# The experts' weight loads issued by ScalarE on a queue of its own, and the last token tile finished in two column halves

## The chip, the cores and the metric

The kernel runs on one core of one Trainium2 chip. The metric is the device time of one execution in microseconds. Before the change three runs took 833.31, 834.32 and 835.25 us, so the median is 834.32 us.

## What is computed

Three blocks follow one another, all in float32, for 2 batches of 576 tokens (1152 tokens) and a model width of 512.

```python
# attention: 8 heads of 64, with a bias that depends on positions
scores = q @ k.T / 8 + bias          # bias[i, j] = relu(log1p|i-j| / log1p(max(i,1)) * w1 + b1) @ w2
attn = softmax(scores); x = attn @ v
# experts: 4 of them, D = 512, F = 1024, every token goes through all, weighted by p
out = sum_e p[:, e] * (relu(x @ w1[e]) @ w2[e])
# gated block: d_ff = 1536
y = ((out @ w_a) * (out @ w_b)) @ w_out
```

## The kernel before, in words

**Numbers.** Matrix products run as three products of a high and a low part (hi*hi, hi*lo, lo*hi), so every operand is split: a cast gives the high part, a subtraction the low part.

**Order.** The order of instructions on each engine is not written down by hand. Every piece of work is an `op` with an estimated cost per engine, a priority (lower goes first) and the buffers it needs. `Plan.run` (line 137) plays the kernel through with these costs when the program is built. Whenever an engine is free in that play, it takes the ready op with the lowest priority whose buffers fit (at equal priority the one that has been ready longest), and the instruction is emitted there and then. On the chip each engine runs its own list in that order, and semaphores make it wait for data and for buffers. DMA transfers are modelled as one line of transfers one after another, at 250 bytes per ns and 1.9 us of latency (`DMA_RATE`, `DMA_LAT`, lines 92 and 93). In that play a DMA costs its issuing engine SyncE (SP) 440 ns. All DMAs of the kernel are issued by SP, so they stand in one hardware queue.

**Stages.** First the bias is made: 36 groups of 16 rows (`bias_group`), each with four hidden-layer tiles `hh` (VectorE L356 or ScalarE L358), eight matmuls `pb` (L370), a copy out of PSUM into `bst` (L388) and a store to a table `bias_d` in DRAM (L405). Attention runs in groups of one or more tiles of 128 query rows (`step`): a tile of bias rows `bt` is loaded from `bias_d` (L458), scores go to `ps` (TensorE L490), VectorE adds the bias and takes the maximum (L493), ScalarE takes the exponential (L503), TensorE transposes the result into `pt` (L516), and `pv` (L581) multiplies by the values. The first eight groups are the 128-row tiles 0 and 1 of the first batch. Tile 1 needs the bias rows up to 255, so it can load only after the sixteenth store.

The experts fill TensorE beside the rest of attention and go on alone after it. Each of 64 units of weights is brought by `unit` (line 615): a 512 KB load into a staging tile `wst` (L617), a cast `wh` (`whi`, on ScalarE or VectorE, L234), a subtraction `wl` (`wlo`, VectorE, L619). There are two staging tiles and, until the bias is finished, four pairs of `w` tiles. So two loads can be in flight, the third load waits until the first staging tile has been read by its `wl`, and no more than six loads can be issued before the first expert product has used its weights. The load has priority 2, the lowest, among SP's ops; the split has priority 1. `early` holds the eighth bias store: in the play no weight load starts before that store has landed. The up products are `up` (L708), the ReLU `hh` and `hl` (L735, L736), the down products `pz` (L719).

The 64-bit weights of the gated block are converted beside the experts and written to DRAM, then read again (`wz_d`). The gated block itself has seven products per pair of blocks (L834), sums on ScalarE and VectorE, and a down product. For the last pair (`out_item`, line 896) the down product of each token tile is emitted in two halves of the inner dimension (L911), then VectorE adds it to the accumulator (L916, 512 columns) and SP stores 256 KB (L920). The last tile, rows 1024 to 1151, is one contiguous run of output rows, so it is one store.

Of the kernel before, what the change touches and what calls it, by code (L numbers as in the profile page):

```python
# [13 lines left out]
ALU = mybir.AluOpType  # L14
# [5 lines left out]
P = 128  # L20
# [21 lines left out]
QUICK, BY_AGE, MARGIN, LATE = 0.9, True, 300, True  # L42
# [46 lines left out]
class Plan:  # L89
# [9 lines left out]
    def op(self, eng, fn, r=(), w=(), rw=(), hold=(), prio=0, lock=False, after=(), size=0):  # L99

        o = Op()
        o.eng, o.fn, o.prio, o.lock, o.size = eng, fn, prio, lock, size
        o.after, o.n, o.done = [], len(self.ops), False
        deps = set(after)
        for b in r:
            deps.update(b.writers)
        for b in rw:
            deps.update(b.writers)
            deps.update(b.readers)
        for b in rw:  # L110
            b.writers, b.readers = [o], []
        for b in w:
            b.writers.append(o)
        for b in r:
            b.readers.append(o)
        deps.discard(o)
        o.left = len(deps)
        for d in deps:
            d.after.append(o)
        o.bufs = list({id(b): b for b in (*r, *w, *rw, *hold)}.values())  # L120
        for b in o.bufs:
            b.left += 1
        self.ops.append(o)
        return o
# [12 lines left out]
    def run(self):  # L137
        ready = {e: [] for e in self.ENG}
        until = dict.fromkeys(self.ENG, 0.0)
        locked = {"DVE": 0.0, "POOL": 0.0}  # L140
        events, now, dma, left, count = [], 0.0, 0.0, len(self.ops), 0
        issued = set()

        def arrive(o, t):
            o.since = t
            for e in o.eng:
                ready[e].append(o)

        for o in self.ops:
            if not o.left:  # L150
                arrive(o, 0.0)
        while left:
            again = True
            while again:
                again = False
                for e in self.ENG:
                    if until[e] > now:
                        continue
                    ready[e] = [o for o in ready[e] if o.n not in issued]
                    best = None  # L160
                    fill = e == "PE" and MARGIN and any(o.prio >= 2 and self.fits(o) for o in ready[e])
                    for o in ready[e]:
                        if best is not None and (o.prio, o.since if BY_AGE else 0, o.n) >= (best.prio, best.since if BY_AGE else 0, best.n):
                            continue
                        if e == "PE" and o.prio < 2 and now < o.since + MARGIN and fill:
                            continue
                        other = {"DVE": "POOL", "POOL": "DVE"}.get(e)
                        if o.lock and other and locked[other] > now:
                            continue

                        if o.prio < QUICK and any(max(until[x], now) + o.eng[x] < now + o.eng[e] for x in o.eng if x != e):
                            continue
                        if self.fits(o):
                            best = o
                    if best is None:
                        continue
                    o = best
                    for b in sorted((b for b in o.bufs if b.t is None), key=lambda b: b.turn):
                        b.place = b.room.free.pop(0)
                        b.room.given += 1  # L180
                        b.t = b.place[0](b.name)
                    o.fn(e)
                    issued.add(o.n)
                    ns = o.eng[e]
                    until[e] = now + ns
                    if e == "SP":
                        dma = max(dma, now + ns + 400) + o.size / self.DMA_RATE
                        end = dma + self.DMA_LAT - 400
                    else:
                        end = now + ns + self.SETTLE[e]  # L190
                        if o.lock and e in locked:
                            locked[e] = now + ns + 50
                    heapq.heappush(events, (until[e], -1, None))
                    heapq.heappush(events, (end, count, o))
                    count += 1
                    again = True
            if not left:
                break
            assert events, ("stuck", [(o.n, list(o.eng), [(b.name, b.t is None) for b in o.bufs]) for e in self.ENG for o in ready[e]][:20])
            now = events[0][0]  # L200
            while events and events[0][0] <= now:
                _, _, o = heapq.heappop(events)
                if o is None:
                    continue
                left -= 1
                o.done = True
                for x in o.after:
                    x.left -= 1
                    if not x.left:
                        arrive(x, now)  # L210
                for b in o.bufs:
                    b.left -= 1
                    if not b.left and b.room is not None:
                        b.room.left -= 1
                        if b.place[1] in b.room.drop:
                            b.room.gone += 1
                        else:
                            b.room.free.append(b.place)
                for x in list(self.watch):
                    if x[0]():  # L220
                        self.watch.remove(x)
                        x[1]()
        return now
# [3 lines left out]
def tile_kernel(ctx, tc, qd, kd, vd, cst, probs, w1r, w2r, war, wbr, wor, out):  # L227
    nc = tc.nc
    plan = Plan()
    op = plan.op  # L230
# [114 lines left out]
    rows, early = [], []  # L345
# [268 lines left out]

    def unit(src):
        wst, w = new("wst"), new("w")
        op({"SP": 440}, lambda e: nc.sync.dma_start(out=wst.t, in_=src.rearrange("p a b -> p (a b)")), w=[wst], prio=2, size=524288, after=early if LATE else [])  # L617
        op(t_copy(1024, ENGINES["whi"]), lambda e: copy(e, w.t[0], wst.t), r=[wst], w=[w], prio=RANK["split"], lock=True)
        op(t_two(1024, ENGINES["wlo"]), lambda e: engine[e].tensor_tensor(out=w.t[1], in0=wst.t, in1=f(w.t[0]), op=ALU.subtract), r=[wst], rw=[w], prio=RANK["split"], lock=True)  # L619
        return w  # L620
# [67 lines left out]
    acc_t, ACC = {}, [Buf(t=x_hi) for _ in range(TOK)]  # L688
    late = {}

    def acc(t):
        if t not in acc_t:
            acc_t[t] = (mid if t < 2 else late["ap"]).tile([P, DM], F32, tag=f"acc{t}", name=f"acc{t}", bufs=1)
        return acc_t[t]
# [201 lines left out]
    def out_item(q, c, h):  # L896
        if (q, "d") not in WU:
            WU[q, "d"] = unit64(UI[q, "d"])
        for tt in range(4 + c):
            t = 4 * c + tt  # L900
            z = new("z", "pz")
            if (q, c) != AB[-1]:
                down(WU[q, "d"], z, h, tt, True, True, after=gap)
            else:

                halves = []
                for ft in (1, 0):
                    def mm(e, ft=ft, z=z, tt=tt):
                        wh, wl = (x.rearrange("p (a b) -> p a b", a=2) for x in WU[q, "d"].t)
                        for j, (a, bb) in enumerate(((h.t[0], wh), (h.t[1], wh), (h.t[0], wl))):  # L910
                            nc.tensor.matmul(z.t, a[:, ft, tt * P:(tt + 1) * P], bb[:, ft, :], start=(ft == 1 and j == 0), stop=(ft == 0 and j == 2))  # L911
                    halves.append(op({"PE": 3 * 226}, mm, r=[WU[q, "d"]], w=[z], hold=[h], prio=RANK["fill"], after=[*parts[q, c, ft], *halves]))
            if q == 0:
                op({"ACT": 600}, lambda e, z=z, t=t: nc.scalar.copy(acc(t), z.t), r=[z], rw=[ACC[t]], prio=RANK["evac2"])
            else:
                op({"DVE": 745}, lambda e, z=z, t=t: nc.vector.tensor_tensor(out=acc(t), in0=z.t, in1=acc(t), op=ALU.add), r=[z], rw=[ACC[t]], prio=RANK["evac2"])  # L916
            if q == NQ - 1:
                def put(e, t=t):
                    for r, o, n in rows_of(t):
                        nc.sync.dma_start(out=out[o:o + n, :], in_=acc(t)[r:r + n])  # L920
                op({"SP": 440 * len(rows_of(t))}, put, r=[ACC[t]], size=262144)
# [174 lines left out]
```

## Time and profile before

| | us |
|---|---|
| median of three runs | 834.32 |
| the profiled execution, its own time | 834.46 |
| its span, first to last instruction | 832.7 |
| TensorE busy (x4890) | 806.7 |
| VectorE busy (x1221) | 626.3 |
| ScalarE busy (x687) | 349.8 |
| GpSimd busy (x72) | 52.1 |
| weight loads `wst<-in_w1r`, `wst<-in_w2r` | 64, 512.0 KB each |

The profile is of one execution. PE is TensorE's matmuls, PEld its weight loads into the array, DVE is VectorE, ACT is ScalarE, SPq is SyncE's sequencer, which issues the DMAs. A row of a timeline gives the start, the length, the engine, the line, the operation and the names of what is written and read; in brackets stands how long the engine had been idle before it and what ended that. The issue of a DMA isn't counted as busy time of its engine. The chain of work that ended last is followed back from the last instruction. It stands for what set the time.

### The profile page before, as it was taken

To read this page: it belongs to the slowest core of one execution; us is meant where nothing else is said; L and a number is where in the kernel's file an instruction comes from. 1 tells how busy PE (TensorE), PEld (TensorE's weight loads), DVE (VectorE), ACT (ScalarE), POOL (GpSimd) and SP (SyncE) were. 2 spreads that over 40 slices of the span, in tenths; PEclk is the share of its full clock that TensorE was granted. 3 is DMA by queue.
4 is the path that set the end of the run, shared out by engine and by line. 5 is a ranking of instruction groups with operands and counts; after the bars stand their busy time and mean duration, and the time that the engine had idled before them with its cause. 6 is when DMAs were issued, how large, how long until landed. Compare 5 with 4: busy or idle time off the path is not lost.

```text
span 832.7 us, 12785 instructions
## 1 busy us (share of the span) xinstructions
PE 806.7 (97%) x4890; PEld 672.2 (81%) x4890; DVE 626.3 (75%) x1221; ACT 349.8 (42%) x687; POOL 52.1 (6%) x72
## 2 busy tenths in 40 slices
PE   7778999999999999999999999999999999999998
PEld 2346776898897788889888988888889999899996
DVE  7998999688888768787888787976266655747545
ACT  6677877477666621132122213113235432324211
POOL 1001100000110000000000000002003001100000
PEclk9999999999999999999999999999999999999999
DMA  6989877675756444556465545640202211211103
GB/s 220 313 285 340 279 256 240 202 235 184 226 176 209 135 159 126 182 174 206 115 202 190 165 140 177 215 127 23 79 1 71 83 58 45 76 27 50 52 1 113
DMA packets 48445, 128.13 MB, mean 154 GB/s; under 512 B 5120, under 2 KB 9216, under 8 KB 48384
## 3 DMA queue, kind: packets, MB, share of 16 engines
q1 hardware_dynamic: 48384, 127.32, 47.5%
q8 instruction: 38, 0.62, 0.3%
q14 instruction: 23, 0.19, 0.1%
HBM read 101.46 MB, written 25.84 MB: 153 GB/s over the span
## 4 chain that ended last, share of the span: by engine, by line
PE 90%; DVE 5%; DMA 3%; ACT 1%; issue 1%; DVEq 0%
PE pz L719 32%; PE up L708 24%; PE pw L834 9%; PE ps L490 5%; PE pv L581 4%; PE pr L834 4%; PE pt L516 4%; PE pq L834 2%; PE pb L370 2%; DMA k<-in_kd 1%; DVE hh L356 1%; DMA bt<-bias_d 1%; PE pz L911 1%; PE px L798 1%; DVE ptb L234 1%
## 5 line engine op out<-in xcount | busy, mean ns | idle before, releaser
L719 PE MATMUL pz<-wh,hh 128*128 128x512 f32 x386 | 153.9, 399 | 0.0
L719 PE MATMUL pz<-wl,hh 128*128 128x512 f32 x386 | 152.3, 395 | 0.0
L719 PE MATMUL pz<-wh,hl 128*128 128x512 f32 x386 | 151.6, 393 | 0.0
L708 PE MATMUL up<-x_hi,wh 128*128 128x256 f32 (+2 forms) x384 | 133.2, 347 | 0.4 <-DVE hl L736 0.4
L708 PE MATMUL up<-x_hi,wl 128*128 128x256 f32 (+2 forms) x384 | 129.8, 338 | 0.0
L708 PE MATMUL up<-x_lo,wh 128*128 128x256 f32 (+2 forms) x384 | 129.7, 338 | 0.0
L735 ACT ACTIVATE hh<-up 128x256 fp32r<-128x256 f32 (+2 forms) x96 | 47.1, 491 | 141.5 <-PE up L708 140.9
L234 ACT CAST wh<-wst 128x1024 fp32r<-128x1024 f32 (+1 forms) x66 | 66.3, 1007 | 93.0 <-PE pz L719 73.7
L719 PEld LDWEIGHTS pz<-wl,hh 128*128 128x128 f32 x386 | 72.5, 188 | 17.2
L619 DVE TENSOR_TENSOR wl<-wst,wh 128x1024 fp32r<-128x1024 f32 x64 | 78.2, 1224 | 10.0 <-ACT wh L234 9.7
L719 PEld LDWEIGHTS pz<-wh,hh 128*128 128x128 f32 x386 | 72.6, 188 | 15.1 <-issue 0.7
L719 PEld LDWEIGHTS pz<-wh,hl 128*128 128x128 f32 x386 | 72.5, 188 | 14.8
L708 PEld LDWEIGHTS up<-x_hi,wh 128*128 128x128 f32 x384 | 72.4, 188 | 9.5 <-issue 1.6
L708 PEld LDWEIGHTS up<-x_lo,wh 128*128 128x128 f32 x384 | 72.4, 189 | 6.4
L708 PEld LDWEIGHTS up<-x_hi,wl 128*128 128x128 f32 x384 | 72.3, 188 | 5.9
L234 ACT COPY ct<-pw 128x512 f32<-128x512 f32 (+3 forms) x48 | 27.8, 579 | 105.5 <-PE pw L834 105.1
L736 DVE SCALAR_TENSOR_TENSOR hl<-up,hh 128x256 fp32r<-128x256 f32 (+2 forms) x96 | 53.0, 554 | 24.1 <-ACT hh L735 23.7
L493 DVE CUSTOM_DVE_ANT_0 pr<-ps,bt 128x576 f32<-128x576 f32 (+1 forms) x80 | 59.7, 754 | 11.4 <-PE ps L490 8.4
L503 ACT ACTIVATE pr<-pr,sums 128x576 f32<-128x576 f32 x72 | 55.9, 776 | 12.7 <-DVE sums L493 11.9
L370 PE MATMUL pb<-hh,cs 128*32 128x288 f32 (+17 forms) x352 | 46.7, 506 | 6.9 <-DVE hh L356 5.4
L356 DVE TENSOR_SCALAR hh<-cs,negb 128x576 f32<-128x576 f32 (+17 forms) x108 | 49.1, 505 | 0.2
L516 PE MATMUL pt<-ident,pr 128*128 128x128 f32 x288 | 43.6, 280 | 2.6 <-ACT pr L503 2.4
(156 smaller groups left out, 1425.5 us busy)
## 6 DMA issues: line engine op xcount, KB each, us to landing
wst<-in_w1r SPq DMA_DIRECT2D x32, 512.0 KB, 4.0
wst<-in_w2r SPq DMA_DIRECT2D x32, 512.0 KB, 4.2
bt<-bias_d SPq DMA_DIRECT2D x24, 576.0 KB, 5.5
bias_d<-bst SPq DMA_DIRECT2D x36, 295.5 KB, 4.7
k<-in_kd SPq DMA_DIRECT2D x16, 576.0 KB, 5.0
v<-in_vd SPq DMA_DIRECT2D x20, 320.0 KB, 4.8
s<-in_war SPq DMA_DIRECT2D x12, 512.0 KB, 5.1
wz_d<-hl SPq DMA_DIRECT2D x24, 256.0 KB, 2.5
```

What stands on the lines that cost most here:

```text
L234: (nc.scalar.copy if e == "ACT" else engine[e].tensor_copy)(out, in_)
L356: op({"DVE": n / 1.92 + 240}, lambda e, hh=hh, G=G: nc.vector.tensor_scalar(out=hh.t[:, :n], in0=tab[:, :n], scalar1=sc[:, G:G + 1], scala ...
L370: nc.tensor.matmul(t[32 * g:32 * g + 32, o + lo:o + hi], w2s, hs[g].t[:, lo:hi], start=True, stop=True)
L493: nc.vector.tensor_tensor_reduce(out=pr.t[r0:r1, c].rearrange("p (a b) -> p a b", a=2), in0=ps.t[r0:r1, :, :HS], in1=bt.t[r0:r1, c].rearra ...
L503: nc.scalar.activation(out=pr.t[:, c], in_=pr.t[:, c], func=AF.Exp, scale=-1.0, bias=sums.t[:, neg:neg + 1], accum_out=sums.t[:, col:col + 1])
L516: nc.tensor.transpose(pt.t[:, kt * P:kt * P + P], pr.t[:, s, k0:k0 + P], ident)
L619: op(t_two(1024, ENGINES["wlo"]), lambda e: engine[e].tensor_tensor(out=w.t[1], in0=wst.t, in1=f(w.t[0]), op=ALU.subtract), r=[wst], rw=[w ...
L708: nc.tensor.matmul(u.t[:, :n], a[:, d, ft * P:(ft + 1) * P], x[:, d, lo:lo + n], start=(d == 0 and j == 0), stop=(d == 3 and j == 2))
L719: nc.tensor.matmul(z.t, a[:, ft, tt * P:(tt + 1) * P], bb[:, ft, :], start=(first and ft == 0 and j == 0), stop=(final and ft == 1 and j = ...
L735: relu = op({"ACT": n / 1.2 + 170}, lambda en, ft=ft, u=u: nc.scalar.activation(out=h.t[0][:, ft, :n], in_=u.t[:, :n], func=AF.Relu), r=[u ...
L736: op({"DVE": n / 0.96 + 160}, lambda en, ft=ft, u=u: nc.vector.scalar_tensor_tensor(out=h.t[1][:, ft, :n], in0=u.t[:, :n], scalar=0.0, in1 ...
L834: nc.tensor.matmul(o_, s[:, k], d[:, k], start=(first and k == 0 and i == 0), stop=(k == 1 and i == 2), skip_group_check=True)
```

## The change

Two things are changed, and one line of the planner that goes with the first.

The 64 loads of expert weights are issued by ScalarE (`nc.scalar.dma_start`) in place of SP. In the planner such a load costs ScalarE 60 ns and has priority 0. The planner's model of a DMA's landing now holds for an op of any engine that has a size.

For the last token tile the second half of the inner dimension is done for columns 0 to 255 and then for columns 256 to 511, six matmuls of 256 columns in place of three of 512. VectorE adds each half of the columns by itself, and each half is stored by itself (128 KB), the first by SP, the second by ScalarE.

```diff
-                    if e == "SP":
+                    if e == "SP" or o.size:
                         dma = max(dma, now + ns + 400) + o.size / self.DMA_RATE
                         end = dma + self.DMA_LAT - 400
...
     def unit(src):
         wst, w = new("wst"), new("w")
-        op({"SP": 440}, lambda e: nc.sync.dma_start(out=wst.t, in_=src.rearrange("p a b -> p (a b)")), w=[wst], prio=2, size=524288, after=early if LATE else [])
+        op({"ACT": 60}, lambda e: nc.scalar.dma_start(out=wst.t, in_=src.rearrange("p a b -> p (a b)")), w=[wst], prio=0, size=524288, after=early if LATE else [])
...
-                halves = []
+                got = []
+                last = tt == 3 + c
                 for ft in (1, 0):
-                    def mm(e, ft=ft, z=z, tt=tt):
...
-                    halves.append(op({"PE": 3 * 226}, mm, r=[WU[q, "d"]], w=[z], hold=[h], prio=RANK["fill"], after=[*parts[q, c, ft], *halves]))
+                    for o, w in ((0, 256), (256, 256)) if last and not ft else ((0, 512),):
+                        def mm(e, ft=ft, z=z, tt=tt, o=o, w=w):
...
+                        got.append(op({"PE": 3 * (w / 2.4 + 13)}, mm, r=[WU[q, "d"]], w=[z], hold=[h], prio=RANK["fill"], after=[*parts[q, c, ft], *got[-1:]]))
+                if last:
+                    for i, g in enumerate(got[1:]):
+                        cols = slice(256 * i, 256 * i + 256)
+                        x = op({"DVE": 430}, lambda e, z=z, t=t, cols=cols: nc.vector.tensor_tensor(out=acc(t)[:, cols], in0=z.t[:, cols], in1=acc(t)[:, cols], op=ALU.add), after=[g, *ACC[t].writers], hold=[z, ACC[t]], prio=RANK["evac2"])
+
+                        def put(e, t=t, cols=cols, i=i):
+                            for r, o, n in rows_of(t):
+                                (nc.sync, nc.scalar)[i].dma_start(out=out[o:o + n, cols], in_=acc(t)[r:r + n, cols])
+                        op({("SP", "ACT")[i]: 440 * len(rows_of(t))}, put, after=[x], hold=[ACC[t]], size=131072)
+                    continue
```

## Rows read from the trace of the kernel before

**Rows 1.** The page, busy time and share of the span.
```profile
PE 806.7 (97%) x4890; PEld 672.2 (81%) x4890; DVE 626.3 (75%) x1221; ACT 349.8 (42%) x687; POOL 52.1 (6%) x72
```
**Rows 2.** By stretch: PE, PEld, DVE, ACT, POOL busy, clock, DMA share, GB/s.
```profile
40.00:57.00 17.00, 14.22 (x161) 9.10 (x159) 16.71 (x47) 13.76 (x32) 0.46 (x1) 1.00 0.83 282
57.00:68.00 11.00, 6.02 (x36) 2.91 (x36) 8.87 (x24) 7.28 (x14) 1.03 (x2) 1.00 1.00 365
...
82.00:295.00 213.00, 211.08 (x1567) 170.94 (x1559) 181.57 (x380) 148.19 (x317) 15.65 (x20) 1.00 0.66 212
295.00:530.00 235.00, 235.00 (x1087) 199.59 (x1086) 192.06 (x328) 51.53 (x77) 3.46 (x2) 1.00 0.56 173
```
**Rows 3.** Waits of PE from 0 to 82 us: total, times, longest.
```profile
PE pb L370 <- DVE hh L356: 5.4, 7, 1.8
PE ps L490 <- DVE sums L493: 4.7, 2, 3.1
```
**Rows 4.** Waits of PE from 82 us to the end.
```profile
PE pw L834 <- DVE ct L859: 1.0, 6, 0.2
PE rp L561 <- ACT ptb L234: 0.9, 1, 0.9
```
**Rows 5.** The chain of work that ended last, around 55 to 66 us: start, length, what.
```profile
54.30 0.40 ACT hh L358
54.70 4.41 DMA bias_d<-bst
...
59.12 7.35 DMA bt<-bias_d
```
**Rows 6.** Timeline of SP, 28 to 62 us: start, length of the issue.
```profile
28.32 0.89 SPq L458 DMA_DIRECT2D bt<-bias_d  x2
...
31.67 0.43 SPq L617 DMA_DIRECT2D wst<-in_w1r  x1
...
54.27 0.33 SPq L617 DMA_DIRECT2D wst<-in_w1r  x1
54.70 0.39 SPq L405 DMA_DIRECT2D bias_d<-bst  x1
...
57.45 0.33 SPq L617 DMA_DIRECT2D wst<-in_w2r  x1
...
59.12 2.42 SPq L458 DMA_DIRECT2D bt<-bias_d  x3
61.60 0.46 SPq L617 DMA_DIRECT2D wst<-in_w1r  x1
```
**Rows 7.** Line 617, whole span: issue ns (least, median, most), first and last start.
```profile
L617 SPq DMA_DIRECT2D wst<-in_w1r x32: 327/328/456, 31.7 to 512.5; - x32
```
**Rows 8.** Waits of SP, whole span: total, times, longest.
```profile
SPq L617 <- DVE wl L619: 118.7, 45, 7.2
```
**Rows 9.** By stretches of 2 us, columns as in rows 2.
```profile
64.00:66.00 2.00, 0.28 (x3) 0.05 (x1) 0.48 (x2) 1.63 (x4) 0.00 (x0) 1.00 1.05 406
...
70.00:72.00 2.00, 2.00 (x10) 1.64 (x9) 1.50 (x7) 1.85 (x5) 0.91 (x1) 0.50 1.07 386
```
**Rows 10.** Timelines of ACT and PE, 205 to 212 us.
```profile
206.07 0.19 ACT L503 ACTIVATION_READ_ACCUMULATOR pr<-pr,sums 128x1 f32 x1
...
208.69 0.60 PE L516 MATMUL pt<-ident,pr 128*128 128x128 f32 x4
```
**Rows 11.** The end: timeline from 828 us.
```profile
827.99 1.37 DVE L916 TENSOR_TENSOR acc<-pz,acc 128x512 f32<-128x512 f32 x2 [0.67 <-PE pz L911]
...
828.24 0.39 PE L911 MATMUL pz<-wl,hh 128*128 128x512 f32 x1
```
**Rows 12.** The last store from issue to landing.
```profile
DMA to landing us min/median/max: 2.4/2.4/2.4
```
**Rows 13.** Stores of 256 KB at 814 to 819 us, each alone in flight.
```profile
DMA to landing us min/median/max: 2.0/2.0/2.0
```
**Rows 14.** Groups by shape, 560 to 832 us: a 256-column sum out of PSUM.
```profile
L850 DVE TENSOR_TENSOR ct<-pq,ct 128x256 f32<-128x256 f32 x12 | 5.1, 424 | 1.7 <-PE pq L834 1.7
```

More of the change, by code (lines that the diff above doesn't have):

```diff
@@ L904, in out_item @@
             else:
-                halves = []
+                got = []
+                last = tt == 3 + c
                 for ft in (1, 0):
-                    def mm(e, ft=ft, z=z, tt=tt):
-                        wh, wl = (x.rearrange("p (a b) -> p a b", a=2) for x in WU[q, "d"].t)
-                        for j, (a, bb) in enumerate(((h.t[0], wh), (h.t[1], wh), (h.t[0], wl))):
-                            nc.tensor.matmul(z.t, a[:, ft, tt * P:(tt + 1) * P], bb[:, ft, :], start=(ft == 1 and j == 0), stop=(ft == 0 and j == 2))
-                    halves.append(op({"PE": 3 * 226}, mm, r=[WU[q, "d"]], w=[z], hold=[h], prio=RANK["fill"], after=[*parts[q, c, ft], *halves]))
+                    for o, w in ((0, 256), (256, 256)) if last and not ft else ((0, 512),):
+                        def mm(e, ft=ft, z=z, tt=tt, o=o, w=w):
+                            wh, wl = (x.rearrange("p (a b) -> p a b", a=2) for x in WU[q, "d"].t)
+                            for j, (a, bb) in enumerate(((h.t[0], wh), (h.t[1], wh), (h.t[0], wl))):
+                                nc.tensor.matmul(z.t[:, o:o + w], a[:, ft, tt * P:(tt + 1) * P], bb[:, ft, o:o + w], start=(ft == 1 and j == 0), stop=(ft == 0 and j == 2), skip_group_check=last)
+                        got.append(op({"PE": 3 * (w / 2.4 + 13)}, mm, r=[WU[q, "d"]], w=[z], hold=[h], prio=RANK["fill"], after=[*parts[q, c, ft], *got[-1:]]))
[8 more added lines that the diff above has]
+                    continue
             if q == 0:
```

## The prediction

> **What bounds the kernel now.** I read the page first: TensorE is busy for 97% of the span [rows 1], so a change that touches no matmul can only win where TensorE stands idle. The windows and TensorE's own waits say where. From 82 us to the end of attention it is busy for 211.1 of 213 us, in the experts' stretch after that for all of it [rows 2], and in the whole time after 82 us its two largest waits come to 1.9 us [rows 4]. Before 82 us it waits 5.4 us for the bias's hidden tiles and 4.7 us for bias additions, one of these 3.1 us long [rows 3]. That long one is the place to look at. In the chain, the sixteenth bias store is issued at 54.70 us and takes 4.41 us to land, and the load of bias rows that waits for it is issued at 59.12 us and takes 7.35 us [rows 5]. Around it the DMA engines are full, share 1.00 at 365 GB/s from 57 to 68 us [rows 2]; TensorE is almost idle from 64 to 66 us, and from 70 to 72 us its granted clock is 0.50, that is 1.2 of 2.4 GHz, after that idle time [rows 9]. So the start is bound by VectorE (16.7 of 17 us busy from 40 to 57 us [rows 2]) and then by the DMA queue, and the rest by TensorE.
>
> **SP's side of the loads.** 64 issues of 0.328 us [rows 7] leave SP, 21.0 us of issue time, and with them SP's waits at these loads, 118.7 us in 45 waits, up to 7.2 us long [rows 8]. What stood behind such a wait were loads of q, k, v and bias rows and bias stores. After 82 us none of that is among TensorE's waits [rows 4], so all of it is worth nothing there: what hides it is a TensorE that is full. In the start one case lies on the chain: the store at 54.70 us stood behind the load issued at 54.27 us [rows 6], and ScalarE is named for the 0.40 us before it [rows 5]. That the store no longer waits is worth 0.4 us; bounds 0 and 0.4.
>
> Do the loads come earlier? 45 of the 64 were waiting for the `wl` that frees their staging tile [rows 8], and that wait moves with them. A queue of its own cannot give a buffer back sooner, so for most loads the time of issue stays what it was. Of the six loads that can be issued before an expert product frees a pair of weight tiles, the first two wait for no buffer. They can go as soon as the planner has seen the eighth store land, about when the first bias rows are loaded at 28.32 us in place of 31.67 us [rows 6].
>
> **ScalarE's side.** ScalarE now spends the issues: no row shows a DMA issued by it. The nearest row is the same load on SP, 0.328 us, at most 0.456 [rows 7]; the other bound is 0, if the issue is hidden behind work that it has already been handed. I take 0.33 us: 21 us in all, 35 of the 64 between 82 and 295 us, so 11.5 us there, where ScalarE is busy for 148 of 213 us, and the others in stretches where it is busy less, 51.5 of 235 us [rows 2]. The planner counts 60 ns, so what stands behind each load comes 0.27 us later than it is planned. Who waits for that: the exponential, then the transposes of `pt`, or ReLU and the down products. In the middle of attention an exponential ends at 206.26 us and the transposes of its turn begin at 208.69 us [rows 10], a reserve of 2.4 us, against 0.33. So the issues cost nothing after 82 us. In the start there are six, 2 us, beside a VectorE that is the fuller engine there; I take nothing for them, bounds 0 and 2 us.
>
> The load also takes its wait to ScalarE. Behind it there stand casts, exponentials and PSUM evacuations. The mean wait on SP was 118.7 / 45 = 2.6 us [rows 8], but SP came early because it had nothing else to do, whereas ScalarE reaches the load only after the work that the planner put ahead of it. Bounds 0 and 2.6 us for each load; I take a wait within the reserve, so 0, and keep the other end for a rival.
>
> **The DMA engines.** The bytes stay the same. One load at the measured rate is 524288 B / 365 GB/s = 1.44 us [rows 2]. The load at 57.45 us stands ahead of the bias rows issued at 59.12 us, and that at 61.60 us behind them [rows 6]. With two queues this order is no longer kept by the queue. If both loads came before 57 us, where the share is 0.83 [rows 2], the bias rows would gain 1.44 us; if the later one took engines from the bias rows, they would lose 1.44. I take 0 and keep both ends, up to 2.9 us each way for the two loads.
>
> The trace before has one data queue and can't show how two of them share. The Trainium skill, DMA: Bandwidth & Descriptors, section "Issuing engines are not separate DMA queues", says that transfers from all issuing engines run on the same 16 DMA engines and that issuing from several saves only the issue time. By that rule the sum would be as I have it, the 0.4 us of the issue path and no more from the second queue; the full share of 1.00 [rows 2] goes with it.
>
> **The end.** The last matmul starts at 828.24 us and runs 0.39; VectorE's last two sums of 512 columns run from 827.99 to 829.36 us [rows 11], the last of them right behind the one before. With two halves it makes two sums of 0.42 us [rows 14] where one of 0.69 was, so the second half is ready some 0.15 us later, as VectorE and not TensorE sets it. The six half-width matmuls stream the same columns. Then the last store is of 128 KB, with half of the bytes, and has its queue to itself. The last store of before took 2.4 us [rows 12], 256 KB alone took 2.0 [rows 13]. No row shows 128 KB alone; between no gain over the last store and the 0.4 for a store alone, plus half of its bytes at 365 GB/s (131072 / 365 = 0.36 us), I take 0.55 us. Less 0.15 that is a gain of 0.4 us, bounds -0.15 (slower) and 0.6.
>
> **The sum.** 0.4 at the store and 0.4 at the end: 0.8 us off the profiled execution's 834.46 us gives 833.7. The median of the runs, 834.32, lies 0.14 us lower, so 833.5 for a median.
>
> **The rivals.** The first: the start gets faster. The two first loads go out three microseconds earlier, the splits follow, and the loads of 54 to 62 us fall into the stretch to 57 us, where engines are free: 17 us at 365 less 282 GB/s is 1.4 MB, or 2.7 loads [rows 2]. The bias rows of 59.12 us then land 1.44 us earlier, the rows behind them up to 2.9, and the 3.1 us wait [rows 3] with its slow clock [rows 9] shrinks by about 2.2 us: 833.5 - 2.2 = 831.3. For it: VectorE and ScalarE need the weights only when their splits come up, and the priority of the load goes from 2 to 0. Against it: the splits keep priority 1, and VectorE has no room before 57 us.
>
> The second ends on the other side: the weights jump the queue. Until now they stood behind whatever SP had issued before. On a queue of their own the first two run beside the first bias rows and the stores, and the last ones beside the bias rows of 59.12 us, with the engines full. The price is two loads, 2.9 us, on the load that takes 7.35 us now; it decides as soon as a weight load is in flight between 59 and 66 us. 833.5 + 2.9 = 836.4. For it: the weights are needed by nobody in that stretch and come at the cost of what is. Against it: one of the two stands ahead already.
>
> The Trainium skill, DMA: Bandwidth & Descriptors, section "Queues, rings and completion order", says that each DMA engine goes round between the queues that it has work for, packet by packet. By it a weight load would take half the engines from bias rows in flight, which is this rival; no row of before shows it.
>
> The third: ScalarE blocks. If a wait at the load exceeds the reserve of 2.4 us in seven of the 35 loads of the attention stretch by 0.5 us, that is 3.5 us: 837.0. For it: 2.6 us of mean wait on SP; against it: the planner sets the load after the buffer is free, and the reserve is as large as that mean. That the change does not do what it says, in that the loads are held by buffers and not by SP, is part of the forecast.
>
> **How the numbers follow.** The three runs span 1.9 us, so about 0.2%, 1.7 us, is what a measurement of this kernel can tell from no change. Chances: forecast 0.38, faster start 0.34, queue jumped 0.18, ScalarE blocked 0.10. All of the planned order is worked out anew by the planner, so that an instruction anywhere may sit elsewhere; this widens each case to both sides by the size of the waits that TensorE still has after 82 us, 1.9 us [rows 4]. A small part of the forecast falls on the faster side, a little of the first rival into no change. Faster by over 0.2%: 0.36; within: 0.37; slower: 0.27. The range for 8 in 10 goes from 830.3, the first rival with a microsecond more, to 837.2, the third rival. The forecast's own range is 832.2 to 835.2.
>
> **What would show it.** Right: 64 loads issued by ScalarE at about 0.33 us, TensorE still full after 82 us, the sixteenth store within 0.5 us of 54.3, a last sum some 0.1 us later and a shorter last store. The first rival: the wait of TensorE for the bias addition under 2 us and no stretch at half clock. The second: bias rows that take over 8 us to land with a weight load in flight. The third: waits of `pt` or `pz` for ScalarE between 82 and 530 us that come to over 2 us. Any of these, or a start whose bias groups come in another order, would make the forecast wrong.

## The result and the profile after

The changed kernel takes 846.76 us, the median of four runs (844.8 to 848.12), beside 834.79 us before (the three runs named above and a fourth): a ratio of 1.0143, 95% interval 1.0129 to 1.0158. It is 12 us slower, and the time lies outside the predicted range. The profiled execution took 846.77 us, with a span of 845.0.

The issues came out as priced. Line 617, over the whole span: least, median and most in ns, then first and last start. It answers [rows 7] and [rows 8].

```profile
L617 ACTq EVENT_SEMAPHORE  x40: 17/17/814, 32.7 to 530.9; - x40
L617 ACTq DMA_DIRECT2D wst<-in_w1r x32: 334/334/462, 24.8 to 524.6; - x32
L617 ACTq DMA_DIRECT2D wst<-in_w2r x32: 334/334/361, 36.6 to 533.8; - x32
```

There are 64 issues of a third of a microsecond, and 40 semaphore instructions ahead of them, of 17 ns in the median and 0.81 us at most. That is not how long ScalarE waits at a load; the part on the steps shows a longer wait. The page's table of DMA queues now has a second data queue, q10, with the 64 loads and the last half store in it (packets, MB, share of 16 engines):

```profile
q1 hardware_dynamic: 39168, 93.63, 34.4%
q10 hardware_dynamic: 9360, 33.69, 12.3%
```

TensorE has as much to do as before and is less busy for its span. The page's busy times, which answer [rows 1]:

```profile
PE 812.3 (96%) x4893; PEld 675.8 (80%) x4893; DVE 632.2 (75%) x1225; ACT 343.4 (41%) x682; POOL 55.3 (7%) x74
```

Where the time went is seen best in three stretches: to 82 us, from there to 295 us (where attention ended before), and the 25 us behind it. The columns are those of [rows 2]: busy time of PE, PEld, DVE, ACT and POOL, granted clock, DMA share, GB/s. The kernel before:

```profile
0.00:82.00 82.00, 63.24 (x490) 34.59 (x490) 72.46 (x184) 57.53 (x113) 8.85 (x21) 0.98 0.84 292
...
295.00:320.00 25.00, 25.00 (x134) 23.36 (x133) 18.28 (x36) 4.49 (x8) 0.00 (x0) 1.00 0.45 147
```

(its middle stretch stands in [rows 2]), and the changed kernel:

```profile
0.00:82.00 82.00, 62.40 (x459) 35.01 (x461) 69.47 (x178) 55.30 (x109) 9.56 (x24) 0.94 0.82 284
82.00:295.00 213.00, 207.63 (x1539) 168.11 (x1537) 187.02 (x380) 140.73 (x306) 15.14 (x16) 1.00 0.67 214
295.00:320.00 25.00, 22.70 (x126) 17.64 (x123) 14.62 (x33) 6.38 (x15) 0.00 (x0) 0.93 0.21 75
```

Two things are read from such rows: the idle time of TensorE (length less busy), and what its clock cost (length times one less the clock). To 320 us TensorE idled 320 - 299.3 = 20.7 us before and 320 - 292.7 = 27.3 us after. The clock cost 82 x 0.02 = 1.6 us before and 82 x 0.06 + 25 x 0.07 = 6.7 us after. Together that is 22.3 against 34.0 us, 11.6 more, and the span is 12.3 us longer. This sum is an estimate: the clock is given in hundredths, and idle time at half clock counts in both terms. By it nearly all of the loss is ahead of 320 us: 4.1 us in the start, 3.5 in the middle, 4.0 at the end of attention. The count (x) shows it too: 1539 matmul records in the middle stretch in place of 1567.

From the end of attention on the lag only travels. The last product with the values (`pv`) begins at 306.7 us in place of 294.6, that is 12.1 us later. Line 581, its matmuls, ns as above, then first and last start, before:

```profile
L581 PE MATMUL pv<-ptb,v x400: 272/379/483, 40.3 to 294.6; 128*64 128x128 f32 x54, 128*64 128x320 f32 x54, 128*64 128x256 f32 x26
```

and after:

```profile
L581 PE MATMUL pv<-ptb,v x400: 272/379/792, 42.5 to 306.7; 128*64 128x128 f32 x54, 128*64 128x320 f32 x54, 128*64 128x256 f32 x26
```

The longest is 792 ns in place of 483. The expert work of the second pass needs all of attention, so TensorE has nothing to put into a gap there. The timeline of PE of the changed kernel shows two waits there, and the half clock behind them:

```profile
293.38 2.91 PE L581 MATMUL pv<-ptb,v 128*64 128x320 f32 x20 [0.56 <-ACT ptb L234]
...
300.52 0.66 PE L516 MATMUL pt<-ident,pr 128*128 128x128 f32 x4 [1.60 <-ACT pr L503]
...
302.10 0.44 PE L561 MATMUL rp<-ident,rx 128*128 128x128 f32 x2 [0.70 <-DVE ptb L234]
...
302.58 4.60 PE L581 MATMUL pv<-ptb,v 128*64 128x320 f32 x20
307.11 0.45 PE L708 MATMUL up<-x_hi,wh 128*128 128x384 f32 x1
```

The twenty matmuls from 302.58 us take 4.60 us. An equal group took 2.91 us nine microseconds earlier, at 293.38 us.

In the start the chain of work that ended last now runs across a weight split (start, length, what):

```profile
32.34 2.36 DVE hh L356 x6
34.70 0.61 DVE wh L234
...
35.34 0.04 DVE wl L619
35.37 1.11 issue
36.48 0.75 DVE pr L493
...
37.27 0.88 ACT pr L503 x2
38.15 0.14 issue
38.28 1.94 PE pt L516 x8
```

Read it from the bottom. The first transposes of attention wait for the exponential, that for the first bias addition `pr`, and the addition stands behind `wh` and `wl` in VectorE's list. The first two weight loads went out at 24.8 us, ahead of the first bias rows, and the planner put their splits first. The kernel before had its first addition 2.7 us earlier:

```profile
33.81 0.75 DVE L493 CUSTOM_DVE_ANT_0 pr<-ps,bt 128x576 f32<-128x576 f32 x1
```

Of these 2.7 us the splits take 1.8, from 34.70 to 36.48 us. The other 0.9 us lie ahead of them: VectorE ends its hidden tiles `hh` only at 34.70 us, and the bias rows land then too (issued at 28.49, 6.2 us on the way). TensorE is idle for 4.38 us, and then it runs at 0.50 of its clock, that is 1.2 of 2.4 GHz (2-us stretches, as [rows 9]):

```profile
36.00:38.00 2.00, 0.00 (x0) 0.00 (x0) 2.00 (x6) 0.73 (x2) 0.00 (x0) 0.59 1.03 399
38.00:40.00 2.00, 1.72 (x8) 1.75 (x9) 1.93 (x4) 1.48 (x5) 0.00 (x0) 0.50 1.06 393
40.00:42.00 2.00, 2.00 (x11) 2.00 (x10) 1.05 (x4) 0.58 (x1) 0.00 (x0) 0.50 1.04 415
```

The obvious reading is that early loads bring early splits, and these bring the stall. The experiments were to show whether that is the 12 us.

### The profile page after: what moved, and what is told of

It reads as the page before. It is cut to its first block, busy times and chain, and to the rows that moved or that the text cites. A ratio compares the mean times of both kernels' runs of the same rounds, so it can differ in the third digit from the quotient of the medians.

```text
span 845.0 us, 12764 instructions
## 1 busy us (share of the span) xinstructions
PE 812.3 (96%) x4893; PEld 675.8 (80%) x4893; DVE 632.2 (75%) x1225; ACT 343.4 (41%) x682; POOL 55.3 (7%) x74
## 3 DMA queue, kind: packets, MB, share of 16 engines
q10 hardware_dynamic: 9360, 33.69, 12.3%
## 4 chain that ended last, share of the span: by engine, by line
PE 83%; DVE 7%; DMA 5%; ACT 3%; issue 1%; SPq 0%; ACTq 0%; DVEq 0%
PE pz L719 30%; PE up L708 22%; PE pw L834 9%; PE ps L490 4%; PE pv L581 4%; PE pr L834 4%; PE pt L516 3%; PE pq L834 2%; DVE hh L356 2%; DMA k<-in_kd 1%; DVE k L443 1%; PE pb L370 1%; DVE pr L493 1%; DMA wst<-in_w2r 1%; ACT pr L503 1%
## 5 line engine op out<-in xcount | busy, mean ns | idle before, releaser
L234 ACT CAST wh<-wst 128x1024 fp32r<-128x1024 f32 (+1 forms) x59 | 59.2, 1004 | 98.3 <-PE pz L719 70.8
L619 DVE TENSOR_TENSOR wl<-wst,wh 128x1024 fp32r<-128x1024 f32 x64 | 77.9, 1221 | 16.2 <-ACT wh L234 15.9
L708 PEld LDWEIGHTS up<-x_hi,wh 128*128 128x128 f32 x384 | 72.3, 188 | 12.2 <-issue 3.7
L234 ACT COPY ct<-pw 128x512 f32<-128x512 f32 (+3 forms) x48 | 27.8, 580 | 105.6 <-PE pw L834 105.1
L234 ACT COPY ptb<-pt 128x512 f32<-128x512 f32 (+3 forms) x92 | 38.5, 441 | 29.1 <-PE pt L516 23.8
```

The costliest lines, as they stand in the source:

```text
L234: (nc.scalar.copy if e == "ACT" else engine[e].tensor_copy)(out, in_)
L708: nc.tensor.matmul(u.t[:, :n], a[:, d, ft * P:(ft + 1) * P], x[:, d, lo:lo + n], start=(d == 0 and j == 0), stop=(d == 3 and j == 2))
```

## The experiments

The change has two effects that can be taken apart. One is who issues a load, and on which queue. The other is where everything stands in the lists, which is the planner's work. A kernel can keep one and change the other.

**The tail alone.** The changed kernel, with line 617 as it was before.

```diff
-        op({"ACT": 60}, lambda e: nc.scalar.dma_start(...), w=[wst], prio=0, ...)
+        op({"SP": 440}, lambda e: nc.sync.dma_start(...), w=[wst], prio=2, ...)
```

> The last token tile in two halves alone, the expert loads as before. If the end gives what the prediction's sum gave it, 0.4 us off: 834.4. If the two halves cost something, for instance because VectorE's second sum and the store from ScalarE come late, up to 1 us more than before: 835.8. Neither theory puts any of the 12 us here.

Measured: 834.63 us, ratio 1.0003 (0.9990 to 1.0016). The halves neither cost nor gain anything.

**The old order with ScalarE's issue.** The kernel before, planned as before, but the instruction goes to ScalarE.

```diff
-        op({"SP": 440}, lambda e: nc.sync.dma_start(...), w=[wst], prio=2, ...)
+        op({"SP": 440}, lambda e: nc.scalar.dma_start(...), w=[wst], prio=2, ...)
```

> The planner plans the loads as SP's, with 440 ns and priority 2, so TensorE, VectorE and GpSimd run the list of before; only the issuing engine is ScalarE. Order theory (the new plan puts attention behind expert work): nothing of the loss, 833.5 to 836. Queue theory (weights on a second queue take the engines from bias rows, and ScalarE is held at the loads): most of the loss, 842 to 847.

Measured: 835.03 us, ratio 1.0007 (0.9995 to 1.0019). The lists of TensorE, VectorE and GpSimd are the same as before, instruction for instruction, and so is ScalarE's but for the loads. So 64 issues on ScalarE, the waits that come with them and the second queue together cost nothing that can be measured.

**The new order with SP's issue.** The reverse: the changed kernel's plan, issued by SP.

```diff
-        op({"ACT": 60}, lambda e: nc.scalar.dma_start(...), w=[wst], prio=0, ...)
+        op({"ACT": 60}, lambda e: nc.sync.dma_start(...), w=[wst], prio=0, ...)
```

> The counterpart: the plan of the changed kernel, with ScalarE's 60 ns and priority 0, and the same lists on TensorE, VectorE and GpSimd, but the load issued by SP. Order theory: as slow as the change, 844 to 848, or slower where SP's own waits are held up by the loads. Queue theory: back to 834 to 837.

Measured: 846.42 us, ratio 1.0144 (1.0125 to 1.0163). The lists of TensorE, VectorE and GpSimd are those of the changed kernel, ScalarE's too but for the loads, there is one data queue, and the whole loss is there. These two runs settle the first half: the loss is in the order of the lists and not in the queue, in the issue or in ScalarE's waits.

**Priority 2 in place of 0.** One number of the changed kernel, `prio=0` to `prio=2` in line 617.

> The change with the load's priority left at 2, so that in the plan a load goes out only when ScalarE has nothing else to do. If the new order is bad because the loads go ahead at priority 0 in the start, this gives most of it back: 834 to 838. If any plan with the loads on ScalarE is bad, 842 to 848.

Measured: 846.92 us, ratio 1.0153 (1.0127 to 1.0179). Giving the priority back doesn't bring the time back.

**Which loads.** Six loads can go before an expert product gives a pair of weight tiles back. The next two kernels divide the loads there, with the tail in halves in both: the first six planned and issued as before and the other 58 as in the change, and the reverse.

```diff
+        if R["wst"].asked <= 6:
+            op({"SP": 440}, lambda e: nc.sync.dma_start(...), w=[wst], prio=2, ...)
+        else:
+            op({"ACT": 60}, lambda e: nc.scalar.dma_start(...), w=[wst], prio=0, ...)
```

> The first six loads, all that can go before an expert product, stay SP's with 440 ns and priority 2; the other 58 are ScalarE's, and the last tile is in two halves. Start theory (the loss comes from early loads whose splits are set ahead of the first attention turns): the start of before, so 834 to 837, with the first expert product near 92 us. Any-plan theory (the order of before is one good draw, and every plan that differs from it loses): 838 to 847.

> The counterpart: the first six loads ScalarE's with priority 0, the other 58 SP's as before. Start theory: most of the 12 us, 843 to 848. If the loss comes from the 58 later loads: 834 to 838. Any-plan theory: anywhere from 838 to 850.

Measured: 838.13 us (1.0034, 1.0020 to 1.0047) with the first six on SP, and 853.18 us (1.0221, 1.0189 to 1.0253) with only these on ScalarE. In these two kernels the first six weigh most, but the parts don't add up: with all 64 moved the loss is 12 us, with six of them moved 18. The first time is at the low edge of the any-plan theory's range, the second above every range.

**Only a later release, nothing on ScalarE.** The kernel before, with the loads held until the tenth bias store, and in a second one until the twenty-first, in place of the eighth.

```diff
-        if u == P // 16 - 1:
+        if u == 9:
             early.append(o)
```

> The kernel before, all loads by SP with priority 2; the planner merely lets the first load go after the tenth bias store in place of the eighth. No ScalarE, no queue, no tail. Any-plan theory: slower than before by 0.5 to 2%, 838 to 850. Start theory: the splits come later, not earlier, so 832 to 836.

> As the last, but after the twenty-first bias store, that is with no weights in the crowded start at all. Start theory: the bias rows meet no weight load, the long wait for the bias addition goes, 829 to 834. Any-plan theory: 838 to 850, or lower by luck.

Measured: 841.23 us (1.0071, 1.0046 to 1.0096) for the tenth, 835.19 us (0.9999, 0.9989 to 1.0010) for the twenty-first. Loads that come a little later cost 6 us, and loads that come much later cost nothing. The start theory missed both (832 to 836 and 829 to 834 us). The any-plan theory had the tenth store, and the twenty-first only by its words "or lower by luck". So a later load isn't a better one by itself.

**Early loads, splits held.** The changed kernel, with the splits held in the plan until the twelfth bias store. It is to take the stall of the start away and leave the loads as early as they are.

```diff
+        if u == 11:
+            held.append(o)
...
-        op(t_copy(1024, ENGINES["whi"]), ..., lock=True)
+        op(t_copy(1024, ENGINES["whi"]), ..., lock=True, after=held)
```

> The changed kernel with one thing added: in the planner the high part of every weight split (L618) also waits for the twelfth bias store, so that VectorE's list again has the first attention groups' bias additions ahead of any split, while the weight loads stay as early on ScalarE's list as in the change. It tells the two things that came with the early loads apart. Theory A (the cost of the start is VectorE's splits ahead of the first attention turns, and the end of attention follows from it): the exponentials of the first four tiles end at 38 to 40 us instead of 44.3, the wait of 4.4 us at 38 us is gone, and the time comes back most of the way, 834 to 839 us. Theory B (the delay of the start is only the first sign; what costs is where the later bias groups and second-batch turns fall in the newly planned order, whose dates any edit of the start shifts): the first turns come back as in A, but the end of attention stays at 300 us or later and the time at 842 to 850 us. Theory C (the loads themselves hold the bias rows up on the engines): the first turns stay late, exponentials of tile 4 end over 42 us, and the time stays at 845 to 848 us.

Measured: 848.36 us, ratio 1.0172 (1.0144 to 1.0201). The chain of that kernel in the start has no split in it any more:

```profile
33.74 0.67 DVE pr L495
...
34.45 0.88 ACT pr L505 x2
35.32 0.14 issue
35.46 0.63 PE pt L518 x4
```

The transposes begin at 35.46 us in place of 38.28, and the first `pv` at 39.0 us, even earlier than before (40.3). Yet the last `pv` begins at the same 306.7 us as in the changed kernel:

```profile
L583 PE MATMUL pv<-ptb,v x400: 272/379/484, 39.0 to 306.7; 128*64 128x128 f32 x54, 128*64 128x320 f32 x54, 128*64 128x256 f32 x26
```

Theory A, the obvious reading above, fell. Its stall is real, but with the stall taken away the time didn't come back. It was lost again in other gaps:

```profile
0.00:82.00 82.00, 62.51 (x478) 35.05 (x478) 69.53 (x178) 57.20 (x108) 12.58 (x27) 0.94 0.82 284
82.00:295.00 213.00, 206.11 (x1501) 166.88 (x1497) 182.42 (x366) 140.55 (x305) 15.54 (x14) 0.99 0.67 216
295.00:320.00 25.00, 23.61 (x143) 18.36 (x142) 17.08 (x41) 8.12 (x22) 0.00 (x0) 1.00 0.19 64
```

The first of these gaps is in the start itself. With idle time and clock counted as above, the stretch to 82 us loses 24.4 us, where the changed kernel loses 24.5. TensorE's longest wait there now ends at 67.88 us and is for a bias addition too (3.1 us at most before [rows 3]):

```profile
PE ps L492 <- DVE sums L495: 6.6, 1, 6.6
```

The middle loses 3.7 us more than in the changed kernel, the end of attention 2.7 less. Theory B had this time (842 to 850 us), and theory C fell with the early transposes. So splits ahead of the first additions aren't needed for the loss. That a stall of the start costs nothing is not shown, as this list has another one.

**The change with a late release.** The changed kernel with `u == 17` in place of the eighth store.

> The changed kernel with the release of the weight loads moved from the eighth bias store to the eighteenth, so that the change's early loads and splits fall behind the first attention turns, all loads still on ScalarE's queue at priority 0, tail in halves. Theory A (early loads and splits are the cost; without them ScalarE's queue is harmless): first turns as before (exponentials of tile 4 end by 40 us), end of attention within 2 us of 295 us, time 832 to 837 us. Theory B (the loads at priority 0 on ScalarE also move the later order, as in the kernel that gave only the first six back to SyncE): first turns as before, end of attention 297 to 302 us, time 837 to 845 us. A time under 832 us would make it the version that beats both kernels.

Measured: 837.14 us, ratio 1.0030 (1.0016 to 1.0045). It gives back 9.6 of the 12 us with all loads on ScalarE, and it doesn't beat the kernel before. The time lies between its two theories, 837 being the edge of both.

**An edit that no instruction carries.** If a newly planned order is itself the cost, it should cost without the change too. One rank of the planner is altered, that of the weight splits, first in the kernel before, then in the changed one.

```diff
-RANK = {..., "split": 1, ...}
+RANK = {..., "split": 0.8, ...}
```

> The kernel before with one number changed that no instruction carries: the planner's rank of the weight splits, 0.8 in place of 1. SyncE loads, eighth store, whole tail, as before; only the order of the lists can differ. Theory A (what costs is the newly planned order itself, and any edit that plans it anew pays or gains about as much): the time is off by more than 0.5% with nothing of the change in it, 839 to 850 us, with TensorE's idle time and half-clock time before 320 us greater by as many us as the span. Theory B (the cost needs the change's early loads or its second queue, and the order before is not special): 833 to 837 us.

> The changed kernel with the planner's rank of the weight splits at 0.8 in place of 1; all else as in the change, loads on ScalarE at priority 0 after the eighth store, tail in halves. Theory A (the order itself): off from the change's 846.8 us by more than 0.5%, to 836 to 843 us, with ScalarE's loads still as early as in the change. Theory B (the early loads or the second queue): 844 to 849 us.

Measured: 846.80 us (1.0155, 1.0118 to 1.0193) in the kernel before, and 843.00 us (1.0113, 1.0084 to 1.0142) in the changed one. The first has SP's loads, the eighth store, the old tail, and the full loss, as its theory A (the order itself) had it. The edit moves work between engines too: VectorE has 1243 instructions in place of 1221, ScalarE 667 in place of 687. The windows of that kernel:

```profile
0.00:82.00 82.00, 62.47 (x474) 34.18 (x478) 71.42 (x182) 55.11 (x108) 9.99 (x22) 0.96 0.83 288
82.00:295.00 213.00, 206.59 (x1521) 166.09 (x1516) 186.94 (x383) 136.76 (x296) 15.37 (x15) 1.00 0.67 214
295.00:320.00 25.00, 22.33 (x132) 18.39 (x129) 16.91 (x37) 7.05 (x18) 0.00 (x0) 1.00 0.23 75
```

The middle loses most, 213 - 206.6 = 6.4 us idle against 1.9 before. For the second, theory A asked for over 0.5% off the change. The ratios, 1.0113 and 1.0143, lie 0.3% apart and their intervals overlap, so this run doesn't decide; its time, 843.00 us, is at the edge of theory A's range.

**All of them in one account.** Idle time and clock cost to 320 us are worked out from the same three rows of each profiled execution, as above. "More" is against before; the first row has the values themselves.

| kernel | idle + clock, us | more | last `pv` begins, more | span, more | median, us |
|---|---|---|---|---|---|
| before | 20.7 + 1.6 | | 294.6 | 832.7 | |
| changed | 27.3 + 6.7 | 11.6 | 12.1 | 12.3 | 846.76 |
| tail alone | 18.5 + 3.3 | -0.6 | -0.4 | -0.3 | 834.63 |
| old order, ScalarE issues | 23.9 + 0 | 1.6 | 2.5 | 2.5 | 835.03 |
| new order, SP issues | 27.5 + 6.7 | 11.9 | 12.0 | 12.2 | 846.42 |
| priority 2 | 26.4 + 8.3 | 12.4 | 12.7 | 12.7 | 846.92 |
| first six on SP | 21.5 + 1.6 | 0.8 | 1.2 | 1.3 | 838.13 |
| only these on ScalarE | 30.5 + 10.6 | 18.7 | 19.3 | 19.4 | 853.18 |
| SP, tenth store | 23.0 + 6.7 | 7.3 | 6.7 | 6.6 | 841.23 |
| SP, twenty-first store | 22.0 + 0 | -0.3 | -2.1 | 0.9 | 835.19 |
| splits held | 27.8 + 7.0 | 12.5 | 12.1 | 12.2 | 848.36 |
| ScalarE, eighteenth store | 22.8 + 1.6 | 2.1 | 2.8 | 2.9 | 837.14 |
| before, rank 0.8 | 28.6 + 3.3 | 9.6 | 11.3 | 11.1 | 846.80 |
| changed, rank 0.8 | 25.1 + 6.6 | 9.3 | 8.0 | 8.9 | 843.00 |

The third column gives the fifth within 1.5 us in every row. Three of the profiled executions lie some 2 us from the median of their kernel (old order with ScalarE's issue: 836.95 against 835.03; first six on SP: 835.86 against 838.13; splits held: 846.69 against 848.36), and their rows are to be read with that. So in every kernel here, up to these 1.5 us, what the span has more is lost by TensorE to gaps and to the half clock before attention ends, whatever it was that changed the plan.

What stays open is why one list leaves more gaps than another. Neither the priority nor the place of the first splits sorts the kernels. The time of the first weight load nearly does. In the six kernels where it goes out by 26.5 us (changed, new order, priority 2, only these on ScalarE, splits held, changed with rank 0.8) the medians are 843.00 to 853.18 us. In the others it goes out at 30.8 us or later, and they take 834.63 to 841.23 us, except the kernel before with rank 0.8: first load at 32.0 us, 846.80 us. So early loads aren't needed for the loss. Whether they are enough for it isn't shown, as no kernel here has early loads and no loss. That a small edit at 25 us moves gaps at 200 and 300 us fits the planner's rule, by which one decision shifts the next; no run follows it from one to the other.

## Why the prediction was wrong

**The step that failed** is in the paragraph on the numbers: the planned order is worked out anew, and that "widens each case to both sides by the size of the waits that TensorE still has after 82 us, 1.9 us [rows 4]". Those rows say how few gaps the old list had. They are no bound on the gaps of another list, because the order that made them so few was being replaced. Nor did it widen the range that was stated: 837.2 is the third rival's 837.0 and 0.2 more. In its place the runs show, over the ten newly planned lists, ratios from 0.9999 to 1.0221: one within 0.2% of before, nine slower, none faster. (The tail alone isn't among them, as its lists are the old ones up to the last token tile, and the new order with SP's issue has the list of the change.) The prediction named what happened, at the end of a paragraph, as an uncertainty that points both ways. It should have been a rival with a price of its own. The rows for such a price were there: TensorE loses only 1.9 of 213 us from 82 to 295 us, so a new order can gain at most about that there, and has far more room to lose.

The same mistake stands behind the other steps: what covered nearly every one was "a TensorE that is full" after 82 us. That fullness is not a property of the work. It is a property of the list, as the kernel before with rank 0.8 shows (6.4 us idle from 82 to 295 us), and the change rewrote the list.

**The steps, one by one.**
- *SP's side, 0.4 us at the sixteenth store:* not confirmed. With the same order the kernel whose loads ScalarE issues is no faster (1.0007). In the changed kernel that store goes out at 61.59 us, 6.9 us later than before.
- *When the loads go:* priced as three microseconds earlier, at about 28.3 us. They went at 24.81 us and the next, 0.4 us later. What held them in the plan was the landing of the eighth bias store, and on the chip ScalarE doesn't wait for it. The first bias rows, which do, go out at 28.49 us.
- *ScalarE's issues, 0.33 us each, nothing on the path:* right, 334 ns each. The waits that they brought to ScalarE were bounded by 2.6 us each, and that is a little short. Ahead of the third load ScalarE stands idle for 2.69 us, until `wl` has read the staging tile:

```profile
33.22 0.68 ACT L358 ACTIVATE hh<-cs 128x368 f32<-128x368 f32 x1
...
35.34 1.23 DVE L619 TENSOR_TENSOR wl<-wst,wh 128x1024 fp32r<-128x1024 f32 x1
...
36.59 0.34 ACTq L617 DMA_DIRECT2D wst<-in_w2r  x1
```

Nothing is held up by it there: the exponential behind it needs the bias addition, which ends at 37.23 us. The third rival, ScalarE blocks, is excluded by the old order with ScalarE's issue.
- *The queue, 0:* right by the same kernel. The page "DMA: Bandwidth & Descriptors" of the Trainium skill, section "Issuing engines are not separate DMA queues", by which a second issuing engine saves issue time and nothing else, agrees with this run: 1.0007.
- *The second rival, weights jump the queue:* something like it is seen. The first tile of bias rows takes 6.2 us to land, where it took 4.1 before. But it takes 5.8 us in the kernel with the new order and one queue, and that kernel loses the same 12 us. The weights are in front because the plan put them there and not because a second queue let them pass.
- *The first rival, a faster start:* against it the prediction said that "VectorE has no room before 57 us". VectorE had no room, and the splits went in all the same, ahead of the first bias additions. "No room" was read as "they won't come early", where it meant "something else will come late".
- *The end, 0.4 us:* not there. VectorE's sums and the last store:

```profile
840.53 0.28 PE L914 MATMUL pz<-wl,hh 128*128 128x256 f32 x1
840.85 0.76 DVE L919 TENSOR_TENSOR acc<-pz,acc 128x256 f32<-128x256 f32 x2
...
841.64 0.35 ACTq L923 DMA_DIRECT2D out<-acc  x1
```

The last sum ends at 841.61 us, 1.08 us behind the start of the last matmul; before it was 829.36 - 828.24 = 1.12 [rows 11]. The last two stores, KB each and us from issue to landing:

```profile
out<-acc SPq DMA_DIRECT2D x1, 128.0 KB, 2.6
out<-acc ACTq DMA_DIRECT2D x1, 128.0 KB, 2.5
```

Half the bytes take 2.5 us where the whole store took 2.4 [rows 12]. The two halves are in flight together; no run shows one alone. The term for the smaller store, 0.55 us, is what was mis-sized: it is nothing. The 0.15 us for a later second half aren't there either.

**The signs.** The prediction's last sign of being wrong, "a start whose bias groups come in another order", came only in part: the bias groups keep their order, but splits and attention's turns stand elsewhere between them. Of the signs of being right, the sixteenth store missed 54.3 us by 7.3. Another failing sign lies in the view that the prediction rested on most. The waits of PE from 82 us to the end, which answer [rows 4]:

```profile
PE ps L490 <- DVE sums L493: 2.7, 4, 1.2
PE pt L516 <- ACT pr L503: 1.8, 2, 1.6
PE pw L834 <- DVE ct L859: 1.0, 6, 0.2
...
PE pt L533 <- ACT ptb L234: 0.3, 1, 0.3
```

Those of `pw` in the gated block are as before, and two waits for attention's turns, which hardly showed before, stand above them.

Two signs came without their rivals. The waits of `pt` for ScalarE come to 1.8 + 0.3 = 2.1 us, over the third rival's 2; the kernel before with rank 0.8 has 2.1 us too, with no weight load on ScalarE. The third tile of bias rows, issued at 29.93 us, takes 9.1 us to land, over the second rival's 8, with a weight load still in flight (7.3 us before); with the new order and one queue it takes 9.9.

## What to carry to other kernels

Where a planner or a scheduler writes the order, an edit of one instruction's engine, cost or priority can replace the whole schedule. Price that first, by how much slack the old schedule has left to give (here 1.9 us) and how much it could lose, and only then the edit itself. To tell the two apart, make both crossed kernels, old order with the new instruction and new order with the old instruction, and one kernel with an edit that no instruction carries. And when a stall has been found at the place where the edit acts, take it away before believing in it, and look where the time went: here it stayed, in part as another stall.

## What the runs showed that was not expected

One idle stretch of TensorE is followed by half clock and another is not. After 4.38 us idle the changed kernel ran at 0.50 from 38 to 42 us. Near its end of attention, from 300 to 302 us, it was busy for 0.88 of 2 us, and 0.50 followed at 304 us (2-us stretches):

```profile
300.00:302.00 2.00, 0.88 (x6) 0.61 (x6) 1.04 (x4) 0.94 (x4) 0.00 (x0) 1.00 0.00 0
...
304.00:306.00 2.00, 2.00 (x10) 0.86 (x8) 0.00 (x0) 0.44 (x1) 0.00 (x0) 0.50 0.00 0
```

The kernel before with rank 0.8 has a gap of that kind at the same place, and its clock stays whole:

```profile
300.00:302.00 2.00, 0.64 (x6) 0.61 (x6) 0.94 (x5) 0.87 (x3) 0.00 (x0) 1.00 0.00 0
302.00:304.00 2.00, 1.30 (x10) 0.65 (x9) 0.72 (x3) 0.93 (x5) 0.00 (x0) 1.00 0.00 0
304.00:306.00 2.00, 2.00 (x18) 1.01 (x14) 0.00 (x0) 0.33 (x1) 0.00 (x0) 1.00 0.00 0
```

So a gap here costs its own length, and sometimes more again: 4 to 5 of the 12 us of the change are clock by the estimate above (6.7 against 1.6 us, of which 0.8 us fell on 36 to 38 us, when TensorE had nothing to run). What decides was not tried.

The other surprise is how little the move itself did. 64 loads of 512 KB changed their engine and their queue, and with the order held the time moved by 0.0007, with an interval that takes in 1.
